# Low-rank attention and a two-layer hard-swish network on one core: transposed scores, sums by a matmul with ones, x kept in SBUF, and the next batch's attention woven between the layers

## The chip, the cores and the metric

One core of one Trainium2 chip runs the whole program. The metric is the device time in microseconds (us), as the median of several runs. A profile of one execution comes with each kernel; its span is some 2 us shorter than the timed run. In the profile PE is the matrix engine, PEld its weight loads, DVE the vector engine, ACT the scalar engine, POOL GpSimd, and L106 is line 106 of that kernel's file. In these kernels PE's products go to tiles in PSUM, the weights and the tiles of k, v, q and x lie in SBUF, and DRAM is the memory that the loads come from.

## The reference, cut to what matters

```python
# attention: batch 8, heads 8, seq 1024, head_dim 64, k_proj 64
k_proj = einsum('ks,bhsd->bhkd', E, k)          # E, F: 64 x 1024
v_proj = einsum('ks,bhsd->bhkd', F, v)
scores = (q @ k_proj^T) / 8;  attn = softmax(scores)      # over 64 columns
x = (attn @ v_proj) transposed to (8192 tokens, 512)
# two layers: 512 -> 2048 -> 512
h = x @ w_in
g = h * clip(h + 3, 0, 6) / 6
out = g @ w_out                                  # 8192 x 512, float32
```

## The kernel before

Attention for all eight batches comes first and writes x to DRAM; then the layers run on blocks of 512 tokens. Inside a batch the probabilities have tokens on partitions, so the row sums are a DVE reduction, and the probabilities have to be divided and then transposed before the product with the values.

```python
kv_pool = tile_pool(name="kv", bufs=1)           # one buffer each for k, q, v
for b in range(B):
    for name, dram in kqv_dram.items():          # rows of 64 floats, 256 bytes
        for so in range(SO):
            load_bf16(t[:, so, :, :], dram[b, :, so])
    ...                                          # projections, q transposes, scores
    nc.scalar.activation(sc_sb[:, h], sc_ps, AF.Exp, scale=scale)
    nc.vector.tensor_reduce(den, sc_sb, axis=AX.X, op=ALU.add)
    nc.vector.reciprocal(den, den)
    nc.vector.tensor_mul(sc_sb, sc_sb, den[:, :, :, None].broadcast_to(...))
    ...                                          # 64 transposes of sc_sb into aT_sb
    nc.tensor.matmul(av_ps, vp_all[:, h, :], aT_sb[...])
    nc.scalar.copy(av_full[:, h, ...], av_ps)
    nc.sync.dma_start(out=xsc_av2[b], in_=av_full)          # x to DRAM
for b in range(B):
    do_moe(b)                                    # reads x from DRAM, and per block:
#   for fo in range(16): 4 matmuls; scalar.copy(h_sb, h_ps);
#       vector.tensor_scalar(t_sb, h_sb, +3, max 0); tensor_scalar(min 6, /6); tensor_mul(g, t_sb, h_sb)
#   for tc_i in range(4): 16 matmuls with g; scalar.copy(o_sb, o_ps); store
```

The softmax here doesn't subtract the row's maximum and nothing guards it: scores larger than these inputs give would overflow.

## Time and profile before

| | before |
|---|---|
| time, median (range) | 749.39 us (748.07 to 750.86) |
| profiled span | 748.0 us |
| attention, until the first layer starts | about 289 us |
| layers, 16 blocks of 28.39 us | about 454 us |
| busy: PE, DVE, ACT, POOL | 80%, 53%, 38%, 24% |
| mean granted clock | 0.906 |

The slices and stretches, which the prediction shows, are read first: they say in which stage an engine is full. Here that is PE, at full clock, in the layers; in attention no engine stays full. Then one reads the chain of waits for the pace of the full stage.

### The profile page before, as it was taken

To read this page: it belongs to the slowest core of one execution; us is meant where nothing else is said; L and a number is where in the kernel's file an instruction comes from. 1 tells how busy PE (TensorE), PEld (TensorE's weight loads), DVE (VectorE), ACT (ScalarE), POOL (GpSimd) and SP (SyncE) were. 2 spreads that over 40 slices of the span, in tenths; PEclk is the share of its full clock that TensorE was granted. 3 is DMA by queue.
4 is the path that set the end of the run, shared out by engine and by line. 5 is a ranking of instruction groups with operands and counts; after the bars stand their busy time and mean duration, and the time that the engine had idled before them with its cause. 6 is when DMAs were issued, how large, how long until landed. Compare 5 with 4: busy or idle time off the path is not lost.

```text
span 748.0 us, 9892 instructions
## 1 busy us (share of the span) xinstructions
PE 597.5 (80%) x3751; PEld 307.4 (41%) x3792; DVE 395.7 (53%) x1040; ACT 283.5 (38%) x513; POOL 180.7 (24%) x220
## 2 busy tenths in 40 slices
PE   0446393663935739999999999999999999999997
PEld 0225263342633524444444444444444444444443
DVE  0146657466584675473473473573563563663652
ACT  0023241632515426354353353353353352452451
POOL 5994676568675600000000000000000000000000
PEclk9986676766867668999999999999999999999999
DMA  9999999999999922211111111111102102101011
GB/s 169 171 155 83 179 145 171 134 132 150 128 154 126 120 57 57 71 42 57 69 44 57 56 57 58 57 43 71 57 32 82 56 29 85 56 30 57 14 43 57
DMA packets 224655, 63.82 MB, mean 85 GB/s; under 512 B 201440, under 2 KB 211680, under 8 KB 224608
## 3 DMA queue, kind: packets, MB, share of 16 engines
q0 software_dynamic: 202720, 29.64, 56.3%
q1 hardware_dynamic: 21888, 33.56, 14.7%
q8 instruction: 29, 0.48, 0.2%
q14 instruction: 18, 0.15, 0.1%
HBM read 67.63 MB, written 25.17 MB: 124 GB/s over the span
## 4 chain that ended last, share of the span: by engine, by line
DVE 31%; PE 27%; issue 4%; ACT 2%; ACTq 0%; DVEq 0%
PE p L119 23%; DVE g_sb L115 14%; DVE t_sb L113 10%; DVE t_sb L111 7%; PE p L106 4%; ACT h_sb L109 1%; ACT av_full L213 1%; ACT sc_sb L189 0%; ACT o_sb L122 0%; ACTq L109 0%; DVEq L115 0%
## 5 line engine op out<-in xcount | busy, mean ns | idle before, releaser
L119 PE MATMUL p<-w_out_sb,g_sb 128*128 128x512 bf16 x1003 | 224.9, 379 | 10.0 <-DVE g_sb L115 8.9
L106 PE MATMUL p<-x_sb,w_in_sb 128*128 128x512 bf16 x1004 | 223.9, 381 | 1.3 <-issue 0.2
L109 ACT CAST h_sb<-p 128x512 bf16<-128x512 f32 x256 | 150.1, 587 | 70.8 <-PE p L106 54.2
L111 DVE TENSOR_SCALAR t_sb<-h_sb 128x512 bf16<-128x512 bf16 x256 | 73.4, 287 | 194.0 <-ACT h_sb L109 193.8
L119 PEld LDWEIGHTS <-g_sb 128*128 128x128 bf16 x1024 | 99.0, 98 | 133.5 <-DVE g_sb L115 18.1
L106 PEld LDWEIGHTS <-w_in_sb 128*128 128x128 bf16 x1024 | 100.5, 98 | 122.5 <-issue 2.8
L201 PE MATMUL p<-ident,sc_sb 128*64 128x128 bf16 x512 | 44.6, 272 | 96.9 <-DVE sc_sb L194 96.9
L115 DVE TENSOR_TENSOR g_sb<-t_sb,h_sb 128x512 bf16<-128x512 bf16 x256 | 108.8, 425 | 9.4
L122 ACT COPY o_sb<-p 128x512 f32<-128x512 f32 x64 | 37.5, 586 | 194.3 <-PE p L119 185.7
L213 ACT CAST av_full<-p 64x512 bf16<-64x512 f32 x128 | 62.6, 616 | 124.6 <-issue 92.6
L201 PEld LDWEIGHTS <-sc_sb 128*64 128x64 bf16 x512 | 43.4, 147 | 97.8 <-DVE sc_sb L194 85.1
L113 DVE TENSOR_SCALAR t_sb<-t_sb 128x512 bf16<-128x512 bf16 x256 | 75.2, 294 | 8.5
L63 POOL DMA_DIRECT2D k<-in_k_dram x64 | 56.3, 934 | 36.8 <-PE p L147 36.7
L63 POOL DMA_DIRECT2D v<-in_v_dram x64 | 56.9, 939 | 27.8 <-DMA k<-in_k_dram 26.8
L189 ACT ACTIVATE sc_sb<-p 128x512 bf16<-128x512 f32 x64 | 32.2, 624 | 71.0 <-PE p L184 49.7
L63 POOL DMA_DIRECT2D q<-in_q_dram x64 | 56.6, 983 | 0.3 <-PE p L201 0.3
L203 DVE COPY aT_sb<-p 64x512 bf16<-64x512 bf16 x128 | 48.4, 412 | 6.5 <-PE p L201 5.9
L192 DVE TENSOR_REDUCE den<-sc_sb 128x64 f32<-128x4096 bf16 x8 | 35.4, 4420 | 24.4 <-ACT sc_sb L189 24.4
L209 PE MATMUL p<-aT_sb,vp_all 64*64 64x512 bf16 x128 | 35.5, 376 | 3.7
L194 DVE TENSOR_TENSOR sc_sb<-sc_sb,den 128x4096 bf16<-128x4096 bf16 x8 | 35.4, 4424 | 0.3
L152 DVE CAST ktp_all<-p 128x64 bf16<-128x64 f32 x32 | 6.9, 224 | 39.7 <-PE p L147 39.7
L155 PE MATMUL p<-v,F_sb 128*64 128x512 bf16 x64 | 24.4, 524 | 2.3 <-DMA v<-in_v_dram 2.3
(28 smaller groups left out, 166.4 us busy)
## 6 DMA issues: line engine op xcount, KB each, us to landing
out_dram<-o_sb SPq DMA_DIRECT2D x64, 256.0 KB, 2.0
k<-in_k_dram POOLq DMA_DIRECT2D x64, 128.0 KB, 9.8
v<-in_v_dram POOLq DMA_DIRECT2D x64, 128.0 KB, 6.3
q<-in_q_dram POOLq DMA_DIRECT2D x64, 128.0 KB, 6.1
x_scratch<-av_full SPq DMA_DIRECT2D x8, 1024.0 KB, 9.2
x_sb<-x_scratch SPq DMA_DIRECT2D x16, 512.0 KB, 3.4
w_in_sb<-in_moe_w_in_dram POOLq DMA_DIRECT2D x4, 512.0 KB, 7.7
w_out_sb<-in_moe_w_out_dram POOLq DMA_DIRECT2D x16, 128.0 KB, 4.9
```

What stands on the lines that cost most here:

```text
L63: nc.gpsimd.dma_start(out=dst, in_=src)
L106: nc.tensor.matmul(h_ps, w_in_sb[:, ko, fo * P:(fo + 1) * P], x_sb[:, ko, :], start=(ko == 0), stop=(ko == KO - 1))
L109: nc.scalar.copy(h_sb, h_ps)
L111: nc.vector.tensor_scalar(t_sb, h_sb, scalar1=3.0, scalar2=0.0, op0=ALU.add, op1=ALU.max)
L113: nc.vector.tensor_scalar(t_sb, t_sb, scalar1=6.0, scalar2=1.0 / 6.0, op0=ALU.min, op1=ALU.mult)
L115: nc.vector.tensor_mul(g_sb[:, fo, :], t_sb, h_sb)
L119: nc.tensor.matmul(o_ps, g_sb[:, fo, tc_i * P:(tc_i + 1) * P], w_out_sb[:, fo, :], start=(fo == 0), stop=(fo == FO - 1))
L122: nc.scalar.copy(o_sb, o_ps)
L201: nc.tensor.transpose(aT_ps[:, ss * P:(ss + 1) * P], sc_sb[:, h, so, :], ident)
L203: nc.vector.tensor_copy(aT_sb[:, h, sg * 4:(sg + 1) * 4, :].rearrange("p a b -> p (a b)"), aT_ps)
L209: nc.tensor.matmul(av_ps, vp_all[:, h, :], aT_sb[:, h, sg * 4:(sg + 1) * 4, :].rearrange("p a b -> p (a b)"), start=True, stop=True)
L213: nc.scalar.copy(av_full[:, h, sg * 512:(sg + 1) * 512], av_ps)
```

## The change

The intent is to take out the serial steps of attention, and to give PE, which is in order and the bound of the layers, an unbroken program in which attention's waits lie behind matmuls of the layers.

```diff
-    "k": k.rearrange("b h (so si) d -> b si so h d", si=P),     # 256-byte rows, 8 transfers, bufs=1
+    "k": k.rearrange("b h (si so) d -> b si h so d", so=SO),    # 2 KB rows, one transfer, bufs=2
...
+  # scores transposed: projected keys on partitions, tokens on the free axis; kb is block-diagonal
+  nc.tensor.matmul(ps, kb[:, 2 * j + a, :], qT[j][:, a, :], start=True, stop=True)
+  nc.scalar.activation(aT[j][:, a, :], ps, AF.Exp, scale=scale)
+  # four 64x64 matmuls on four different quarters of the array
+  for t in range(NB):
+      for a in range(2):
+          r, c = t * KP, a * D
+          nc.tensor.matmul(tiles[t][c:c + D], stationary(r, 2 * j + a), aT[j][r:r + KP, a, :], ...)
+  den = quads(lambda r, h: ones[r:r + KP, :], j);  av = quads(lambda r, h: vp[r:r + KP, h, :], j)
+  # 1/den as exp(-ln(den)) on ACT, one product on DVE, x stays in SBUF
+  nc.scalar.activation(lns[t], den[t], AF.Ln)
+  nc.scalar.activation(rec, ln, AF.Exp, scale=-1.0)
+  nc.vector.tensor_mul(xT[:, j, t, :], av, rec)
...
-  nc.scalar.copy(h_sb, h_ps)                    # then three DVE passes
+  nc.scalar.activation(r, h_ps, AF.Relu, bias=half[:], scale=1.0 / 6.0)
+  nc.vector.scalar_tensor_tensor(g[:, fo, :], r, 1.0, h_ps, op0=ALU.min, op1=ALU.mult)
...
+  for t in range(NB):                           # two blocks per batch
+      for fo in range(FO):
+          first_group(xT, t, g, fo)
+          next(steps, None)                     # one step of the next batch's attention
+          if prev is not None and fo % SB == SB - 1:
+              second_group(*prev, fo // SB)     # a quarter of the block before
+              next(steps, None)
+      prev = (b, t, g)
```

Instructions are issued in the order of the program text; no scheduler moves them. The order of the loads is: k, v, q of batch 0, w_in, w_out, k, v, q of batch 1.

More of the change, by code (lines that the diff above doesn't have):

```diff
@@ L12 @@
 ALU = mybir.AluOpType
-AX = mybir.AxisListType
 @with_exitstack
@@ L38 @@
     FO = d_ff // P
-    x_scratch = nc.dram_tensor("x_scratch", (B, d_model, S), bf16, kind="Internal").ap()
-    k_v = k.rearrange("b h (so si) d -> b h si so d", si=P)
-    v_v = v.rearrange("b h (so si) d -> b h si so d", si=P)
-    q_v = q.rearrange("b h (so si) d -> b so si h d", si=P)
+    TOK = 512
+    NB = S // TOK
+    SB = SO // NB
+    kqv_dram = {
+        "k": k.rearrange("b h (si so) d -> b si h so d", so=SO),
+        "v": v.rearrange("b h (si so) d -> b si h so d", so=SO),
+        "q": q.rearrange("b h (si so) d -> b si h so d", so=SO),
+    }
@@ L45 @@
     w_in_v = moe_w_in.rearrange("(ko ki) n -> ki ko n", ki=P)
-    w_out_v = moe_w_out.rearrange("(ko ki) n -> ki ko n", ki=P)
-    x_scratch_v = x_scratch.rearrange("b (ko ki) t -> b ki ko t", ki=P)
-    xsc_av = x_scratch.rearrange("b (h d) (sc si) -> b d h sc si", d=D, si=P)
+    w_out_v = moe_w_out.rearrange("(fo ki) n -> ki fo n", ki=P)
+    out_v = out.rearrange("(b si so) m -> b si so m", si=P, so=SO)
     consts = ctx.enter_context(tc.tile_pool(name="consts", bufs=1))
-    psum = ctx.enter_context(tc.tile_pool(name="psum", bufs=8, space=bass.MemoryType.PSUM))
@@ L54, in ps @@
-    def ps(pp, ff, dt=f32):
-        t = psum.tile([P, 512], f32, tag="p", name="p")
-        if dt != f32:
-            t = t.bitcast(dt)
-        return t[:pp, :ff]
-    _LETTERS = "abcdefgh"
-    def load_bf16(dst, src, eng=None, pool=None, sz=512):
-        nc.gpsimd.dma_start(out=dst, in_=src)
-    ident = consts.tile([P, P], bf16)
-    make_identity(nc, ident)
-    E_sb = consts.tile([P, SO, KP], bf16)
-    F_sb = consts.tile([P, SO, KP], bf16)
-    w_in_sb = consts.tile([P, KO, d_ff], bf16)
@@ L71 @@
-    w_out_sb = consts.tile([P, FO, d_model], bf16)
-    for ko in range(KO):
-        load_bf16(w_in_sb[:, ko, :], w_in_v[:, ko, :], sz=2048)
-    for fo in range(FO):
-        load_bf16(w_out_sb[:, fo, :], w_out_v[:, fo, :], sz=2048)
-    E_raw = consts.tile([KP, SO, P], bf16)
-    F_raw = consts.tile([KP, SO, P], bf16)
-    load_bf16(E_raw, E.rearrange("kp (so si) -> kp so si", si=P), sz=2048)
-    load_bf16(F_raw, F.rearrange("kp (so si) -> kp so si", si=P), sz=2048)
-    for so in range(SO):
-        tp = ps(P, KP, bf16)
-        nc.tensor.transpose(tp, E_raw[:, so, :], ident[:KP, :KP])
-        nc.vector.tensor_copy(E_sb[:, so, :], tp)
-        tp = ps(P, KP, bf16)
-        nc.tensor.transpose(tp, F_raw[:, so, :], ident[:KP, :KP])
-        nc.vector.tensor_copy(F_sb[:, so, :], tp)
@@ L89 @@
-    kv_pool = ctx.enter_context(tc.tile_pool(name="kv", bufs=1))
-    proj_pool = ctx.enter_context(tc.tile_pool(name="proj", bufs=2))
-    work_pool = ctx.enter_context(tc.tile_pool(name="work", bufs=2))
-    av_pool = ctx.enter_context(tc.tile_pool(name="av", bufs=2))
-    moe_x = ctx.enter_context(tc.tile_pool(name="moe_x", bufs=3))
-    moe_g = ctx.enter_context(tc.tile_pool(name="moe_g", bufs=1))
-    moe_o = ctx.enter_context(tc.tile_pool(name="moe_o", bufs=4))
-    TOK = 512
-    def do_moe(b):
-        for tblk in range(S // TOK):
-            x_sb = moe_x.tile([P, KO, TOK], bf16, tag="x_sb")
-            nc.sync.dma_start(out=x_sb[:], in_=x_scratch_v[b, :, :, tblk * TOK:(tblk + 1) * TOK])
-            g_sb = moe_g.tile([P, FO, TOK], bf16, tag="g_sb")
-            for fo in range(FO):
-                h_ps = ps(P, TOK)
-                for ko in range(KO):
-                    nc.tensor.matmul(h_ps, w_in_sb[:, ko, fo * P:(fo + 1) * P], x_sb[:, ko, :],
-                                     start=(ko == 0), stop=(ko == KO - 1))
-                h_sb = moe_o.tile([P, TOK], bf16, tag="hb")
-                nc.scalar.copy(h_sb, h_ps)
-                t_sb = moe_o.tile([P, TOK], bf16, tag="hs")
-                nc.vector.tensor_scalar(t_sb, h_sb, scalar1=3.0, scalar2=0.0,
-                                        op0=ALU.add, op1=ALU.max)
-                nc.vector.tensor_scalar(t_sb, t_sb, scalar1=6.0, scalar2=1.0 / 6.0,
-                                        op0=ALU.min, op1=ALU.mult)
-                nc.vector.tensor_mul(g_sb[:, fo, :], t_sb, h_sb)
-            for tc_i in range(TOK // P):
-                o_ps = ps(P, d_model)
-                for fo in range(FO):
-                    nc.tensor.matmul(o_ps, g_sb[:, fo, tc_i * P:(tc_i + 1) * P],
-                                     w_out_sb[:, fo, :], start=(fo == 0), stop=(fo == FO - 1))
-                o_sb = moe_o.tile([P, d_model], f32, tag="o_sb")
-                nc.scalar.copy(o_sb, o_ps)
-                tok_lo = b * S + tblk * TOK + tc_i * P
-                nc.sync.dma_start(out=out[tok_lo:tok_lo + P, :], in_=o_sb)
@@ L126 @@
-    NPAIR = H // 2
-    kqv_dram = {
-        'k': k.rearrange("b h (so si) d -> b si so h d", si=P),
-        'v': v.rearrange("b h (so si) d -> b si so h d", si=P),
-        'q': q.rearrange("b h (so si) d -> b si so h d", si=P),
-    }
-    xsc_av2 = x_scratch.rearrange("b (h d) s -> b d h s", d=D)
-    for b in range(B):
-        kqv = {}
-        for name, dram in kqv_dram.items():
-            t = kv_pool.tile([P, SO, H, D], bf16, tag=name, name=name)
-            for so in range(SO):
-                load_bf16(t[:, so, :, :], dram[b, :, so])
-            kqv[name] = t
-        k_sb, v_sb, q_sb = kqv['k'], kqv['v'], kqv['q']
-        ktp_all = proj_pool.tile([P, NPAIR, KP], bf16, tag="ktp")
-        vp_all = proj_pool.tile([KP, H, D], bf16, tag="vp")
-        for j in range(NPAIR):
-            ktp_ps = ps(P, KP)
-            for so in range(SO):
-                nc.tensor.matmul(
-                    ktp_ps,
-                    k_sb[:, so, 2 * j:2 * j + 2, :].rearrange("p h d -> p (h d)"),
-                    E_sb[:, so, :],
-                    start=(so == 0), stop=(so == SO - 1))
-            nc.vector.tensor_copy(ktp_all[:, j, :], ktp_ps)
-        vp_ps = ps(KP, H * D)
-        for so in range(SO):
-            nc.tensor.matmul(
-                vp_ps,
-                F_sb[:, so, :],
-                v_sb[:, so, :, :].rearrange("p h d -> p (h d)"),
-                start=(so == 0), stop=(so == SO - 1))
-        nc.vector.tensor_copy(vp_all.rearrange("k h d -> k (h d)"), vp_ps)
-        av_full = av_pool.tile([D, H, S], bf16, tag="av")
-        qT_sb = work_pool.tile([P, NPAIR, SO, P], bf16, tag="qT")
-        sc_sb = work_pool.tile([P, H, SO, KP], bf16, tag="sc")
-        aT_sb = work_pool.tile([KP, H, SO, P], bf16, tag="aT")
-        den = work_pool.tile([P, H, SO], f32, tag="den")
-        for j in range(NPAIR):
-            for sg in range(2):
-                qT_ps = ps(P, 512, bf16)
-                for ss in range(4):
-                    so = sg * 4 + ss
-                    nc.tensor.transpose(
-                        qT_ps[:, ss * P:(ss + 1) * P],
-                        q_sb[:, so, 2 * j:2 * j + 2, :].rearrange("p h d -> p (h d)"),
-                        ident)
-                nc.vector.tensor_copy(
-                    qT_sb[:, j, sg * 4:(sg + 1) * 4, :].rearrange("p a b -> p (a b)"),
-                    qT_ps)
-        for h in range(H):
-            j, hl = h // 2, h % 2
-            off = hl * D
-            sc_ps = ps(P, SO * KP)
-            for so in range(SO):
-                nc.tensor.matmul(
-                    sc_ps[:, so * KP:(so + 1) * KP],
-                    qT_sb[off:off + D, j, so, :],
-                    ktp_all[off:off + D, j, :],
-                    start=True, stop=True)
-            nc.scalar.activation(
-                sc_sb[:, h], sc_ps.rearrange("p (so k) -> p so k", so=SO),
-                AF.Exp, scale=scale)
-        nc.vector.tensor_reduce(den, sc_sb, axis=AX.X, op=ALU.add)
-        nc.vector.reciprocal(den, den)
-        nc.vector.tensor_mul(sc_sb, sc_sb,
-                             den[:, :, :, None].broadcast_to([P, H, SO, KP]))
-        for h in range(H):
-            for sg in range(2):
-                aT_ps = ps(KP, 512, bf16)
-                for ss in range(4):
-                    so = sg * 4 + ss
-                    nc.tensor.transpose(aT_ps[:, ss * P:(ss + 1) * P],
-                                        sc_sb[:, h, so, :], ident)
-                nc.vector.tensor_copy(
-                    aT_sb[:, h, sg * 4:(sg + 1) * 4, :].rearrange("p a b -> p (a b)"),
-                    aT_ps)
-        for h in range(H):
-            for sg in range(2):
-                av_ps = ps(D, 512)
-                nc.tensor.matmul(
-                    av_ps, vp_all[:, h, :],
-                    aT_sb[:, h, sg * 4:(sg + 1) * 4, :].rearrange("p a b -> p (a b)"),
-                    start=True, stop=True)
-                nc.scalar.copy(av_full[:, h, sg * 512:(sg + 1) * 512], av_ps)
-        nc.sync.dma_start(out=xsc_av2[b], in_=av_full)
@@ L216 @@
-    for b in range(B):
-        do_moe(b)
+    kqv_pool = ctx.enter_context(tc.tile_pool(name="kqv", bufs=2))
+    att = ctx.enter_context(tc.tile_pool(name="att", bufs=2))
+    xpool = ctx.enter_context(tc.tile_pool(name="x", bufs=2))
+    gpool = ctx.enter_context(tc.tile_pool(name="g", bufs=2))
+    rpool = ctx.enter_context(tc.tile_pool(name="r", bufs=4))
+    opool = ctx.enter_context(tc.tile_pool(name="o", bufs=3))
+    ps_mm = ctx.enter_context(tc.tile_pool(name="ps_mm", bufs=4, space=bass.MemoryType.PSUM))
@@ new lines, with pmm, pat @@
+    ps_at = ctx.enter_context(tc.tile_pool(name="ps_at", bufs=4, space=bass.MemoryType.PSUM))
+    ctx.enter_context(tc.manual_schedule())
+    def pmm():
+        return ps_mm.tile([P, TOK], f32, tag="mm", name="mm")
+    def pat():
+        return ps_at.tile([P, TOK], f32, tag="at", name="at")
+    nc.scalar.preload_act_table_set("natural_log_exp_and_others")
+    ef_raw = consts.tile([P, S], bf16, name="ef_raw")
+    nc.gpsimd.dma_start(out=ef_raw[:KP], in_=E)
+    nc.gpsimd.dma_start(out=ef_raw[KP:], in_=F)
@@ new lines, in load, with load_kqv @@
+    def load(b, name):
+        t = kqv_pool.tile([P, H, SO, D], bf16, tag=name, name=name)
+        nc.gpsimd.dma_start(out=t, in_=kqv_dram[name][b])
+        return t
+    def load_kqv(b):
+        return {n: load(b, n) for n in ("k", "v", "q")}
+    ident = consts.tile([P, P], bf16, name="ident")
+    make_identity(nc, ident)
+    ones = consts.tile([P, D], bf16, name="ones")
+    nc.vector.memset(ones, 1.0)
+    half = consts.tile([P, 1], f32, name="half")
+    nc.vector.memset(half, 0.5)
+    kbd = [consts.tile([P, H, P], bf16, name=f"kbd{i}") for i in range(2)]
@@ new lines @@
+    for t in kbd:
+        nc.vector.memset(t, 0.0)
+    kqv = {0: load_kqv(0)}
+    w_in_sb = consts.tile([P, KO, d_ff], bf16, name="w_in_sb")
+    w_out_sb = consts.tile([P, FO, d_model], bf16, name="w_out_sb")
+    NW = 4
+    for i in range(NW):
+        c = slice(i * d_ff // NW, (i + 1) * d_ff // NW)
+        nc.gpsimd.dma_start(out=w_in_sb[:, :, c], in_=w_in_v[:, :, c])
+    for i in range(NW):
+        c = slice(i * FO // NW, (i + 1) * FO // NW)
+        nc.gpsimd.dma_start(out=w_out_sb[:, c, :], in_=w_out_v[:, c, :])
@@ new lines, with attention, project, q_transpose @@
+    kqv[1] = load_kqv(1)
+    ef_t = consts.tile([P, 2, SO, 2, KP], bf16, name="ef_t")
+    ef_si = ef_raw.rearrange("r (si so) -> r so si", so=SO)
+    ef_ps = pat().bitcast(bf16)
+    for so in range(SO):
+        nc.tensor.transpose(ef_ps[:, so * P:(so + 1) * P], ef_si[:, so, :], ident)
+    ef_pv = ef_ps.rearrange("p (so e r) -> p e so r", so=SO, e=2)
+    for e in range(2):
+        for a in range(2):
+            nc.vector.tensor_copy(ef_t[:, e, :, a, :], ef_pv[:, e])
+    def attention(b, xT):
+        kt, vt, qt = kqv[b]["k"], kqv[b]["v"], kqv[b]["q"]
+        kb = kbd[b % 2]
+        def project(e, src):
+            ps = pat()
+            for so in range(SO):
+                nc.tensor.matmul(ps, ef_t[:, e, so].rearrange("p a m -> p (a m)"), src[:, :, so, :],
+                                 start=(so == 0), stop=(so == SO - 1))
+                if so == SO // 2 - 1:
+                    yield
+            res[e] = ps
+        res = {}
+        yield from project(0, kt)
+        kp = att.tile([KP, H, 2, D], bf16, tag="kp", name="kp")
+        k_ps = res[0].rearrange("p (h d) -> p h d", h=H)
+        for a in range(2):
+            nc.vector.tensor_copy(kp[:, :, a, :], k_ps[:KP])
+        yield
+        yield from project(1, vt)
+        vp = att.tile([P, H, D], bf16, tag="vp", name="vp")
+        nc.vector.tensor_copy(vp.rearrange("p h d -> p (h d)"), res[1])
+        yield
+        kt_ps = pat().bitcast(bf16)[:, :H * KP]
+        for h in range(H):
+            nc.tensor.transpose(kt_ps[:, h * KP:(h + 1) * KP], kp[:, h].rearrange("p a d -> p (a d)"),
+                                ident[:KP, :KP])
+        kt_ps = kt_ps.rearrange("p (h m) -> p h m", h=H)
+        nc.vector.tensor_copy(kb[:D, :, :KP], kt_ps[:D])
+        nc.vector.tensor_copy(kb[D:, :, KP:], kt_ps[D:])
+        yield
+        qT, aT = {}, {}
+        def q_transpose(j):
+            ps = pat().bitcast(bf16)
+            for a in range(2):
+                for m in range(SB):
+                    o = (a * SB + m) * P
+                    nc.tensor.transpose(ps[:, o:o + P],
+                                        qt[:, 2 * j + a, 2 * m:2 * m + 2, :].rearrange("p s d -> p (s d)"),
+                                        ident)
+            qT[j] = att.tile([P, 2, TOK], bf16, tag="qT", name="qT")
+            nc.vector.tensor_copy(qT[j].rearrange("p a n -> p (a n)"), ps)
+        def scores(j):
+            aT[j] = att.tile([P, 2, TOK], bf16, tag="aT", name="aT")
+            for a in range(2):
+                ps = pat()
+                nc.tensor.matmul(ps, kb[:, 2 * j + a, :], qT[j][:, a, :], start=True, stop=True)
+                nc.scalar.activation(aT[j][:, a, :], ps, AF.Exp, scale=scale)
+        def quads(stationary, j):
+            tiles = [pat() for t in range(NB)]
+            for t in range(NB):
+                for a in range(2):
+                    r, c = t * KP, a * D
+                    nc.tensor.matmul(tiles[t][c:c + D], stationary(r, 2 * j + a),
+                                     aT[j][r:r + KP, a, :], start=True, stop=True)
+            return tiles
+        def values(j):
+            den = quads(lambda r, h: ones[r:r + KP, :], j)
+            av = quads(lambda r, h: vp[r:r + KP, h, :], j)
+            lns = []
+            for t in range(NB):
+                lns.append(att.tile([P, TOK], f32, tag="ln", name="ln"))
+                nc.scalar.activation(lns[t], den[t], AF.Ln)
+            return av, lns
+        def normalise(j, t, av, ln):
+            rec = att.tile([P, TOK], f32, tag="rec", name="rec")
+            nc.scalar.activation(rec, ln, AF.Exp, scale=-1.0)
+            nc.vector.tensor_mul(xT[:, j, t, :], av, rec)
+        q_transpose(0)
+        yield
+        for j in range(KO):
+            scores(j)
+            yield
+            if j + 1 < KO:
+                q_transpose(j + 1)
+            yield
+            yield
+            av, lns = values(j)
+            yield
+            for t in range(NB):
+                normalise(j, t, av[t], lns[t])
+                yield
@@ new lines, in first_group, with second_group @@
+    def first_group(xT, t, g, fo):
+        h_ps = pmm()
+        for ko in range(KO):
+            nc.tensor.matmul(h_ps, w_in_sb[:, ko, fo * P:(fo + 1) * P], xT[:, ko, t, :],
+                             start=(ko == 0), stop=(ko == KO - 1))
+        r = rpool.tile([P, TOK], f32, tag="r", name="r")
+        nc.scalar.activation(r, h_ps, AF.Relu, bias=half[:], scale=1.0 / 6.0)
+        nc.vector.scalar_tensor_tensor(g[:, fo, :], r, 1.0, h_ps, op0=ALU.min, op1=ALU.mult)
+    def second_group(b, t, g, c):
+        o_ps = pmm()
+        for fo in range(FO):
+            nc.tensor.matmul(o_ps, g[:, fo, c * P:(c + 1) * P], w_out_sb[:, fo, :],
+                             start=(fo == 0), stop=(fo == FO - 1))
+        o_sb = opool.tile([P, d_model], f32, tag="o_sb", name="o_sb")
+        nc.scalar.copy(o_sb, o_ps)
+        nc.sync.dma_start(out=out_v[b, :, NB * c + t, :], in_=o_sb)
@@ new lines, in x_tile @@
+    def x_tile():
+        return xpool.tile([P, KO, NB, TOK], bf16, tag="xT", name="xT")
+    xT = x_tile()
+    for _ in attention(0, xT):
+        pass
+    prev = None
+    for b in range(B):
+        steps = iter(())
+        if b + 1 < B:
+            x_next = x_tile()
+            steps = attention(b + 1, x_next)
+        if b + 2 < B:
+            kqv[b + 2] = load_kqv(b + 2)
+        for t in range(NB):
+            g = gpool.tile([P, FO, TOK], bf16, tag="g", name="g")
+            for fo in range(FO):
+                first_group(xT, t, g, fo)
[4 more added lines that the diff above has]
+            prev = (b, t, g)
+        for _ in steps:
+            pass
+        if b + 1 < B:
+            xT = x_next
@@ L221 @@
+    for c in range(SB):
+        second_group(*prev, c)
 _INS = ['q', 'k', 'v', 'E', 'F', 'moe_w_in', 'moe_w_out']
```

## The prediction

> **What bounds the kernel now.** I read the slices of the page first, then the busy time by stretches, then the chain of waits in order of time, then the groups by form, then the waits. The slices show two stages:
>
> ```profile
> PE   0446393663935739999999999999999999999997
> DVE  0146657466584675473473473573563563663652
> ACT  0023241632515426354353353353353352452451
> POOL 5994676568675600000000000000000000000000
> PEclk9986676766867668999999999999999999999999
> DMA  9999999999999922211111111111102102101011
> ```
>
> Attention for all eight batches comes first, then the two layers. The stretches (PE, weight load, DVE, ACT, POOL, clock, DMA, GB/s):
>
> ```profile
> 20.00:22.00 2.00, 0.00 (x0) 0.00 (x0) 0.00 (x0) 0.00 (x0) 1.64 (x4) 1.00 1.24 202
> 35.00:40.00 5.00, 3.50 (x6) 0.65 (x5) 0.05 (x1) 0.00 (x0) 5.00 (x7) 1.00 2.43 155
> 100.00:150.00 50.00, 30.16 (x365) 20.35 (x363) 28.07 (x48) 23.31 (x48) 32.56 (x38) 0.75 1.74 149
> 400.00:450.00 50.00, 48.55 (x222) 21.84 (x225) 29.71 (x96) 22.29 (x38) 0.00 (x0) 1.00 0.16 53
> ```
>
> Up to about 289 us no engine is full and the granted clock is about 0.75: loads in 256-byte rows, one buffer for k, q and v, and a serial chain inside a batch. After that PE is 97% busy at full clock. The chain gives the pace there:
>
> ```profile
> 375.28 0.88 PE p L106 x4
> 403.67 0.88 PE p L106 x4
> 432.06 0.88 PE p L106 x4
> 534.89 10.53 PE p L119 x48
> ```
>
> One block of 512 tokens takes 403.67 - 375.28 = 28.39 us, and 16 blocks take 454 us. The last row gives the pace of one full matmul, (10.53 - 0.38) / 47 = 0.216 us, where 0.38 is the latency of the last. 128 of them are 27.65, so 0.74 of a block is waiting, mostly for the last g_sb. The durations I use (busy, mean ns):
>
> ```profile
> L109 ACT CAST h_sb<-p 128x512 bf16<-128x512 f32 x256 | 150.1, 587 | 70.8 <-PE p L106 54.2 <-DVE t_sb L113 8.3 <-DVE g_sb L115 4.2
> L189 ACT ACTIVATE sc_sb<-p 128x512 bf16<-128x512 f32 x64 | 32.2, 624 | 71.0 <-PE p L184 49.7 <-issue 21.3
> L160 DVE CAST vp_all<-p 64x512 bf16<-64x512 f32 x8 | 5.5, 683 | 24.2 <-PE p L155 24.2
> L176 DVE COPY qT_sb<-p 128x512 bf16<-128x512 bf16 x64 | 22.2, 408 | 4.8 <-PE p L172 4.7
> ```
>
> And from the timeline, 32 transposes at full clock, (1.96 - 0.23) / 31 = 0.056 us each, and the wait that attention's serial chain puts on PE:
>
> ```profile
> 262.61 1.96 PE L172 MATMUL p<-ident,q 128*128 128x128 bf16 x32
> PE p L201 <- DVE sc_sb L194: 96.9, 8, 12.6
> ```
>
> **What the Trainium skill says.** "TensorE: Matmul & The Clock Gate", Part 1: a clock gate follows recent activity, half rate after an idle window of about 3.4 us and full after a busy one. The trace agrees: 0.75 in attention, 1.00 in the layers. So woven attention should run at full clock. "TensorEngine Tiling (Array Packing)", Tiling Modes and Key Properties: a 64x64 shape is four independent tiles, and a change of mode drains the array. The trace has 64x64 matmuls, but all on one tile, so it shows neither. "DMA: Bandwidth & Descriptors", Specifications: rows under 512 B do not reach line rate. The trace agrees: 155 GB/s written with 256-byte source rows, 202 with the 2 KB rows of w_out. "ScalarE: Activation LUTs", Table sets: one set holds both exp and ln. The built program has one table load; the kernel before uses no ln, so it shows nothing more.
>
> **The change, part by part.**
> Removed: the 96.9 us in which PE waits for the division by row sums, the transposes of the probabilities, the trip of x through DRAM, and DVE's three passes per group (0.29 + 0.29 + 0.42 us) for one that reads PSUM.
>
> Layers: 2048 full matmuls stay. With the second layer one block behind, the 0.74 us per block should vanish: 2048 x 0.216 = 442.4 us.
>
> Attention on PE, per batch: two projections, 16 x 0.216 = 3.46; the key transposes, 8 of 64 columns, about 0.03 each, 0.25; the q transposes, 32 x 0.056 = 1.79; the scores, 8 x 0.216 = 1.73; sums and values, 32 matmuls of 64x64, in groups of four different tiles. One after the other they are 32 x 0.216 = 6.91; perfectly overlapped 1.73. I take pairs, 3.46 (my estimate, as the weight loads of two tiles in the same rows may block each other). Entering and leaving the small mode 8 times costs the latency beyond the pace, 0.38 - 0.216 = 0.16, so 1.3. Sum 12.0 us, on the path for the seven woven batches: 84.0.
>
> Start: batch 0's attention, batch 1's loads. The queue carries in order E and F (0.26 MB written), k, v, q of batch 0 (3.15), both weights (4.19), and k, v, q of batch 1 (3.15), in all 10.75 MB. At 201 GB/s from 2.5 us on (first bytes in the trace), plus 1.1 us to the semaphore (E_raw landed at 25.1 after 4.33 MB), q of batch 1 lands at 53.5 + 2.5 + 1.1 = 57 us. Batch 0's q lands near 23 us; its attention, four head pairs at about 4.7 us (six activations of 0.62 and one round through PE), ends near 44. Then PE's program needs k of batch 1 after the first group of layer one, at about 47, v after the third, q after the sixth. PE runs in program order, so by 57 it has done only 24 matmuls of the layers, the projections and the key transposes of batch 1. From there it should not stop.
>
> Sum: 57 + (2048 - 24) x 0.216 = 437 + (84.0 - 3.7) = 80 + end 4 (the last matmul before started at 744.0 of 748.0) + 3 for a cold clock when PE restarts + 4 for local waits = 585 us.
>
> ACT and DVE lie beside this. ACT: 256 + 8 x 24 activations of 0.62 and 64 copies of 0.59 make 316 us. DVE: 256 passes of 0.69, per batch 8 products of 0.69, three PSUM casts of 0.68, two copies of 0.41 and four of 0.66 (1024 wide) make 265 us. Both are under 60% of the span.
>
> **Rivals.**
> 1. The four tiles run one after another. For it: no overlap is seen before. Against: the skill. It adds 7 x 3.45 = 24, so 609; full overlap takes off 12, so 573.
> 2. The start is longer, because the large kqv loads move at the old 155 GB/s: 10.75 MB take 69 us in place of 53.5, so 600. Against: w_out has the same 2 KB rows and got 202.
> 3. DVE takes the place of PE locally: in the two normalising steps of a head pair it has 2 x 0.69 us against 0.865 of PE, so it falls 1 us behind, 28 times, and PSUM fills: up to +28, so 613. Against: four PSUM buffers are 2.6 us of lead, and every fourth group is followed by 3.5 us of second-layer matmuls without DVE work.
> 4. Attention hides entirely, as if the layers had idle PE time to fill: 57 + 437 + 10 = 504. Against: PE is 97% busy there, so every woven matmul lengthens the path.
>
> **Range and chances.** The large gain is safe: 289 us of attention become about 57 of start and 80 of woven matmuls. Overlap (-12 to +24), DMA rate (up to +15) and local waits (-4 to +15) give the range 565 to 612. They rarely all go one way. Faster by over 2% has 0.98.
>
> **What would show it.** PE busy over 95% and clock 1.00 from about 60 us to the end; PE waiting for k, v, q loads before 60; layer matmuls still 0.216 apart; the group of eight sum and value matmuls taking about 0.9 us (1.7 if serial, 0.45 to 0.6 if overlapped); 64 to 68 us per batch in the steady part and 55 in the last, which has no attention; PE waits for PSUM released by DVE under 10 us. Wrong if PE's longest waits in the steady part are on DVE or ACT, or if the loads of batch 1 land after 65.

## The result

The changed kernel takes 575.71 us (574.86 to 576.98, 4 runs) against 749.39 (748.07 to 750.86, 4 runs). The ratio is 0.7688, with a 95% interval of 0.7668 to 0.7707. Ratios are the mean time of one kernel's fast runs over that of the other's in the same rounds, so not quite the ratio of the medians. Run again later on another occasion it took 576.09 (ratio 0.7693); differences below are against that.

The slices after, in the order of the page:

```profile
PE   2656999999999999999999999999999999999997
DVE  1342764354535454535544454345444544444420
ACT  0261876366644665356743576437653666544431
PEclk9887999999999999999999999999999999999999
DMA  9999992552419150380507333000110000011011
```

A slice is now 14.3 us. Four slices of start are left; after them PE is full and the clock is full. In stretches (PE, PEld, DVE, ACT, POOL, clock, DMA, GB/s) there are the bad piece of the start, one whole batch with attention woven in, and the last batch, which has none:

```profile
40.00:50.00 10.00, 1.79 (x5) 0.69 (x6) 0.69 (x1) 0.59 (x1) 0.00 (x0) 0.50 1.24 207
218.30:284.56 66.26, 65.10 (x346) 29.64 (x352) 31.39 (x49) 37.52 (x66) 2.63 (x3) 1.00 0.41 80
496.45:551.71 55.26, 55.00 (x253) 25.05 (x256) 22.03 (x33) 26.68 (x40) 0.00 (x0) 1.00 0.10 39
```

The difference of the last two rows, 66.26 - 55.26 = 11.0 us, is what attention costs per batch. The 55.26 are 256 matmuls at 0.216. The period is the distance between equal pieces in the chain of waits, here of the second layer:

```profile
218.30 2.75 PE mm L223 x12
284.56 2.75 PE mm L223 x12
350.82 2.75 PE mm L223 x12
417.08 2.75 PE mm L223 x12
```

PE's timeline around the end of batch 0's attention (start, duration, engine, line; the dots stand for rows left out) shows the standstill:

```profile
37.28 0.97 PE L214 MATMUL mm<-xT,w_in_sb 128*128 128x512 bf16 x2 [0.16 <-issue]
39.28 0.58 PE L214 MATMUL mm<-xT,w_in_sb 128*128 128x512 bf16 x1 [1.04 <-DVE xT L193]
48.21 1.89 PE L126 MATMUL at<-k,ef_t 128*128 128x512 bf16 x4 [8.34 <-DMA k<-in_k_dram]
...
53.33 1.04 PE L126 MATMUL at<-v,ef_t 128*128 128x512 bf16 x4
...
58.37 0.62 PE L159 MATMUL at<-ident,q 128*128 128x128 bf16 x8
```

The bracket at the end of the third row tells what came before it: 8.34 us idle until k of batch 1 has landed. Everything earlier is loads and batch 0's attention. The last two rows are the first work on v and q of batch 1. Each starts within 0.1 us of its landing, which the trace puts at 53.29 and 58.32. In the steady part, one visit to the sums and values (the eight small matmuls of a head pair) looks like this:

```profile
207.14 0.41 PE L177 MATMUL at<-aT,ones 64*64 64x512 bf16 x4
207.38 0.39 PE L177 MATMUL at<-aT,vp 64*64 64x512 bf16 x4
207.70 1.90 PE L214 MATMUL mm<-xT,w_in_sb 128*128 128x512 bf16 x7
```

Four matmuls with 512 columns each start and give way to the next four within 0.24 us, where one after another they would need 4 x 0.216 = 0.86. The groups that took the place of the three DVE passes, and the longest PE wait for another engine:

```profile
L218 DVE SCALAR_TENSOR_TENSOR g<-r,mm 128x512 bf16<-128x512 f32 x256 | 175.5, 686 | 227.4 <-ACT r L217 226.8
L217 ACT ACTIVATE r<-mm,half 128x512 f32<-128x512 f32 x256 | 176.8, 691 | 73.6 <-PE mm L214 72.0
PE at L169 <- DVE qT L163: 6.2, 8, 0.8
```

DVE is idle for long stretches in front of its group, waiting for ACT, and ACT in front of its own, waiting for PE, so neither is the bound. The last row says that PE waits for DVE's first copy of q once per batch, 6.2 us in the whole run.

### The profile page after: what moved, and what is told of

It reads as the page before. It is cut to its first block, busy times and chain, and to the rows that moved or that the text cites. A ratio compares the mean times of both kernels' runs of the same rounds, so it can differ in the third digit from the quotient of the medians.

```text
span 573.1 us, 7173 instructions
## 1 busy us (share of the span) xinstructions
PE 532.7 (93%) x2770; PEld 240.3 (42%) x2824; DVE 254.4 (44%) x400; ACT 302.9 (53%) x513; POOL 28.9 (5%) x40
## 4 chain that ended last, share of the span: by engine, by line
PE 86%; DMA 8%; DVE 2%; ACT 1%; issue 1%; POOL 1%; ACTq 0%; POOLq 0%
PE mm L223 38%; PE mm L214 37%; DMA v<-in_v_dram 4%; PE at L126 4%; DMA w_in_sb<-in_moe_w_in_dram 4%; PE at L177 3%; PE at L169 2%; PE at L159 2%; DVE g L218 1%; ACT r L217 1%; DVE qT L163 1%; PE at L145 0%; POOL v L78 0%; POOL q L78 0%; POOL k L78 0%
## 5 line engine op out<-in xcount | busy, mean ns | idle before, releaser
L218 DVE SCALAR_TENSOR_TENSOR g<-r,mm 128x512 bf16<-128x512 f32 x256 | 175.5, 686 | 227.4 <-ACT r L217 226.8
L214 PE MATMUL mm<-xT,w_in_sb 128*128 128x512 bf16 x982 | 241.2, 381 | 3.0 <-DVE xT L193 1.0
L223 PE MATMUL mm<-w_out_sb,g 128*128 128x512 bf16 x1012 | 230.0, 379 | 0.6
L217 ACT ACTIVATE r<-mm,half 128x512 f32<-128x512 f32 x256 | 176.8, 691 | 73.6 <-PE mm L214 72.0
L223 PEld LDWEIGHTS <-g 128*128 128x128 bf16 x1024 | 99.8, 98 | 119.3
L226 ACT COPY o_sb<-mm 128x512 f32<-128x512 f32 x64 | 37.5, 587 | 164.7 <-PE mm L223 161.9
L193 DVE TENSOR_TENSOR xT<-at,rec 128x512 bf16<-128x512 f32 x64 | 43.5, 685 | 22.1 <-ACT rec L192 22.1
L192 ACT ACTIVATE rec<-ln 128x512 f32<-128x512 f32 x64 | 40.6, 641 | 0.0
L126 PE MATMUL at<-k,ef_t 128*128 128x512 bf16 x64 | 18.8, 426 | 14.4 <-DMA k<-in_k_dram 14.4
L78 POOL DMA_DIRECT2D k<-in_k_dram x8 | 7.0, 881 | 140.6 <-PE at L126 137.0
L78 POOL DMA_DIRECT2D q<-in_q_dram x8 | 7.0, 880 | 140.1 <-PE at L159 136.0
```

The lines of the kernel that those rows point to most:

```text
L126: nc.tensor.matmul(ps, ef_t[:, e, so].rearrange("p a m -> p (a m)"), src[:, :, so, :], start=(so == 0), stop=(so == SO - 1))
L192: nc.scalar.activation(rec, ln, AF.Exp, scale=-1.0)
L193: nc.vector.tensor_mul(xT[:, j, t, :], av, rec)
L214: nc.tensor.matmul(h_ps, w_in_sb[:, ko, fo * P:(fo + 1) * P], xT[:, ko, t, :], start=(ko == 0), stop=(ko == KO - 1))
L217: nc.scalar.activation(r, h_ps, AF.Relu, bias=half[:], scale=1.0 / 6.0)
L218: nc.vector.scalar_tensor_tensor(g[:, fo, :], r, 1.0, h_ps, op0=ALU.min, op1=ALU.mult)
```

## The experiments

The theory to be tested: the time is the start, until PE has data for an unbroken program, plus PE's program in order at 0.216 us per full matmul; what the other engines and the DMA do beside it is hidden. Its rivals: the gain is that of the removed work, and the weaving matters little; or another engine is already about to be the bound.

All runs gave the right result. Times are medians of four runs; "more" or "less" is against 576.09. The experiments were run on three occasions, each on another chip, and the kernel before, timed beside them, took 749.71, 748.68 and 747.80 us. So a difference of under 2 us between runs of different occasions says little.

### Weaving undone

```diff
-            steps = attention(b + 1, x_next)
+            for _ in attention(b + 1, x_next):
+                pass
```

> The next batch's attention is issued whole ahead of the batch's layers, not woven in; everything else as in the changed kernel. Theory: the work on PE is the same 11 us per batch, but each batch now shows its chain through ACT and DVE: about 15 us from q transposes to the last product as in batch 0 plus 7 to 9 for projections, so 12 to 14 us more for each of 7 batches, and colder clock: 655 to 675. Rival (the gain came from the removed work, not from the weaving): under 600.

Measured: 647.44 us, ratio 0.8654, so 71 us more; somewhat less than the expected range. One period, with attention alone and then the layers alone:

```profile
192.99:212.95 19.96, 15.28 (x97) 6.46 (x97) 9.35 (x15) 11.73 (x23) 2.62 (x3) 0.78 0.88 139
212.95:268.76 55.81, 55.54 (x250) 25.17 (x255) 23.28 (x34) 27.45 (x42) 0.00 (x0) 0.99 0.16 45
```

Attention by itself takes 20.0 us at a clock of 0.78, woven in it costs 11.0. Per period that is 75.77 - 66.26 = 9.5 us, 67 in seven batches. The expectation had taken 7 to 9 us for the projections and 15 for the chain from the q transposes on. In the trace the first part takes 3.9 us (192.99 to 196.87) and the second 16.1, so the shortfall lies in the projections. Of the 173 us between the two kernels, about 71 come from the weaving, as measured by taking it out of the finished kernel. The other 102 come without it, from the removed work and the other parts together.

### Four small tiles made into full matmuls

Zero-padded weights of 128x128, two matmuls accumulating into each output, so the same count of instructions and the same result. The padding costs three more small DVE copies per batch.

```diff
-  nc.tensor.matmul(tiles[t][c:c + D], stationary(r, 2 * j + a), aT[j][r:r + KP, a, :], start=True, stop=True)
+  nc.tensor.matmul(tiles[t], stationary(t, a), aT[j][:, a, :], start=(a == 0), stop=(a == 1))
```

> The sums and values without small tiles: zero-padded 128x128 weights, the same 32 matmuls per batch, two accumulating into each output, same result. Theory: eight of them take 8 x 0.216 = 1.73 us instead of the 0.56 in the trace, 4 x 7 times on PE's path: +33 us, about 608. Rival (PE has waits in the attention steps that the longer matmuls fill): less than +15.

Measured: 605.74 us, ratio 0.8077, 30 more. The same visit in its trace, and two pieces that give its period:

```profile
219.16 1.03 PE L192 MATMUL at<-aT,ones 128*128 128x512 bf16 x4
220.02 1.03 PE L192 MATMUL at<-aT,vbd 128*128 128x512 bf16 x4
220.88 1.89 PE L229 MATMUL mm<-xT,w_in_sb 128*128 128x512 bf16 x7
...
232.54 2.75 PE mm L238 x12
303.06 2.75 PE mm L238 x12
```

The visit takes 1.72 us in place of 0.56, and the period is 70.52, 4.26 more, 29.8 in seven batches. PE's path explains the whole difference, and the extra DVE copies do not lie on it: PE's waits for qT are 6.9 us, against 6.2. It is a little less than 28 x 1.16 = 32.5, because the small visits also cost some 0.09 us before they begin, which the full ones do not.

### The sums issued twice

```diff
-            for t in range(NB):
+            for t in list(range(NB)) * times:      # times = 2 for the sums
```

> The four small matmuls of the sums are issued twice per head pair, with the same result. Theory (four tiles overlap, 0.24 us per four): 28 x 0.24 = +6.7, about 582.5. Rival (they run one after another, and the trace's spacing is a drawing): 28 x 0.86 = +24, about 600.

Measured: 581.55 us, ratio 0.7779, 5.5 more. Four more small matmuls in each of 28 woven visits cost 0.2 us each time, so the overlap is real and not a drawing of the profile.

### The loads of batch 1 ahead of the second layer's weights

```diff
+    kqv[1] = load_kqv(1)
     for i in range(NW):
         nc.gpsimd.dma_start(out=w_out_sb[:, c, :], in_=w_out_v[:, c, :])
-    kqv[1] = load_kqv(1)
```

> Only change: k, v, q of batch 1 are loaded ahead of w_out instead of behind it. Theory (the time is the start until PE has its data, plus PE's program in order): the three tensors land 10.5 us earlier, PE no longer stands still from 39.9 to 48.2 us and w_out still arrives before its first use at about 63, so 9 to 11 us less than 575.7: about 566. Rival (the start is bound by batch 0's own attention and its activations, the loads lie beside it): at most 3 us less, above 572.

Measured: 567.33 us, ratio 0.7573, 8.8 less, just under the expected 9 to 11. PE waits for k only once, for batch 0's, at the very start (6.9 us; in the changed kernel two waits, 14.4). Batch 1's first projection now starts at 41.70, right behind batch 0's last wait (41.32), so it is batch 0's attention that bounds the start from here.

### The same, and one empty step in each batch

```diff
         q_transpose(0)
         yield
+        yield
         for j in range(KO):
```

> The same reordering, and one empty step more between the first q transposes and the first scores of every batch, so that the DVE copy of qT is done when PE comes to it. Theory: the 0.79 us wait per batch goes away, 7 times, so about 5 us less than the reordering alone: 560. Rival: the wait only moves to a later step or PSUM, no difference to the reordering alone (within 1.5 us).

Measured: 561.24 us, ratio 0.7487, 6 less again. Its only wait for qT is that of batch 0, and its period is 65.40:

```profile
PE at L169 <- DVE qT L163: 0.8, 1, 0.8
...
204.14 2.59 PE mm L215 x12
269.54 2.59 PE mm L215 x12
```

This version beats both kernels: 15 us, 2.7% less than the changed one (0.7487 / 0.7693 = 0.973).

### x through DRAM again

x of each batch is written to DRAM and read back before the layers take it, first for all batches, then for all but batch 0.

```diff
+            nc.sync.dma_start(out=x_scratch[b, t], in_=x[:, :, t, :])
+            nc.sync.dma_start(out=y[:, :, t, :], in_=x_scratch[b, t])
```

> x goes to DRAM and back between attention and the layers, as in the kernel before, all else as changed. Theory: the trip of batch b+1 is begun with some eight steps of batch b to spare, about 15 us or more, and takes 5 to 12 us, so it is hidden except for batch 0, where it adds its latency of about 10 us less what the wait for batch 1's loads at 48 us hides: 0 to +5, so 576 to 581. Rival (the DRAM trip was a cost in itself): +15 or more, with PE waiting for x at every batch.

Measured: 588.31 us, ratio 0.7856, 12 more: a miss. The period stayed at 66.26, but PE stood still in the start:

```profile
PE mm L216 <- DMA x<-x_scratch: 21.4, 2, 20.0
...
40.67 1.29 SPq L237 DMA_DIRECT2D x_scratch<-xT  x2
49.86 4.72 SPq L239 DMA_DIRECT2D x<-x_scratch  x2
```

The second pair of rows is the queue of the transfers: the write of x was issued at 40.67, and the read could only be issued at 49.86, when the write had landed; the data came at 58.8. The DMA was full of batch 1's loads at that time, so each of the two halves of x (512 KB) was slow: the first took 9.2 us to DRAM and 8.9 us back. I had put the whole trip at 10.

> x through DRAM and back for batches 1 to 7, batch 0 direct. In the run with all batches the period stayed at 66.26 us and the start alone lost 20 us in a wait for x behind the bulk loads. Theory: the trip is hidden for the later batches, within 2 us of the changed kernel, 574 to 578. Rival (the trip costs in the steady part too): +10 or more.

Measured: 578.27 us, ratio 0.7729, 2.2 more, just outside what was expected; the period is again 66.26. There is one wait for x of 1.6 us. In the steady part, where no bulk load is under way, the read could be issued 3.4 us after the write (158.21 to 161.59), against 9.2 in the start. So keeping x in SBUF is worth nothing that these runs show in the steady part, once attention is a batch ahead, and some 10 us in the start.

### Short rows in the loads

```diff
-        "k": k.rearrange("b h (si so) d -> b si h so d", so=SO),
+        "k": k.rearrange("b h (so si) d -> b si h so d", so=SO),     # and 8 transfers per tensor
```

> k, q and v loaded in 256-byte rows by 8 transfers each, as in the kernel before, tokens in the old order. Theory: only the start sees it: 6.3 MB at 155 in place of 207 GB/s are 10 us more before v of batch 1 is there, +8 to +12, about 586; GpSimd is busy 7 us per tensor but off the path. Rival (the loads also disturb the steady part through DMA or GpSimd): +25 or more, and a period longer than 66.3 us per batch.

Measured: 588.09 us, ratio 0.7856, 12.0 more, at the upper edge of the range. The period is 66.26 (431.02 to 497.28 in its chain), although GpSimd was busy 176 us in place of 29. So the large loads with long rows are worth something in the start alone.

The run changes two things at once, the rows and the number of transfers, and the trace speaks for the second, against the expectation's "off the path". GpSimd needs 7.05 us to issue the eight transfers of k, and between 60 and 75 us it is busy 14.63 of 15.00 us. At some 0.87 us for 128 KB, issuing alone gives 151 GB/s (my estimate from these figures), and 144 to 146 were moved while GpSimd was full. In the kernel before, the 24 transfers of batch 0 (issued from 21.4 to 41.5 us) each land some 5 us after their issue, the last no later than the first, as if none had to queue. Longer rows in as many transfers were not tried, so this stays open.

### The lag of the second layer, and the three passes

First the lag alone undone: the second layer follows its own block's first.

```diff
-                if prev is not None and fo % SB == SB - 1:
-                    second_group(*prev, fo // SB)
-                    next(steps, None)
+            for c in range(SB):
+                second_group(b, t, g, c)
+                next(steps, None)
```

> The second layer directly behind its own block's first layer, not one block behind; the attention steps are called as often, first 16 and then 4 in a block. Theory: PE stands still once a block until the last g is there (ACT 0.69, DVE 0.69, latency, about 1.3 us; it was 0.6 to 0.74 in the kernel before), 16 times: +12 to +22 us, 588 to 598; DVE falling behind in the now denser first layer can add to that. Rival (attention steps fill that gap): under +5.

Measured: 579.4 us, ratio 0.7744, 3.3 more. The theory's number is a miss, and the rival's is right, though for another reason, which I saw only now. The second layer takes g in order, and its last matmul of the first quarter comes 15 x 0.216 = 3.2 us after its first. The last g needs only some 1.4 us (0.69 on ACT and 0.69 on DVE). There is nothing to wait for, with or without a lag, as long as DVE keeps up, and this run's trace has no wait of PE for g. So I undid the single pass, with and without the lag.

```diff
-        nc.scalar.activation(r, h_ps, AF.Relu, bias=half[:], scale=1.0 / 6.0)
-        nc.vector.scalar_tensor_tensor(g[:, fo, :], r, 1.0, h_ps, op0=ALU.min, op1=ALU.mult)
+        nc.scalar.copy(h_sb, h_ps)
+        nc.vector.tensor_scalar(t_sb, h_sb, scalar1=3.0, scalar2=0.0, op0=ALU.add, op1=ALU.max)
+        nc.vector.tensor_scalar(t_sb, t_sb, scalar1=6.0, scalar2=1.0 / 6.0, op0=ALU.min, op1=ALU.mult)
+        nc.vector.tensor_mul(g[:, fo, :], t_sb, h_sb)
```

> Only the step between the layers undone: ACT copies PSUM to bf16 and DVE makes three passes (0.29, 0.29 and 0.42 us, 1.0 in all against 0.69), second layer still one block behind. Theory (every fourth group is followed by 3.5 us of second-layer matmuls, in which DVE catches up, and PSUM buffers hold the rest): within +3 of the changed kernel, 574 to 579. Rival (DVE, with 1.0 us against PE's 0.865 per group plus attention's share, becomes the bound in the woven steps): +15 or more.

Measured with the lag: 580.76 us, ratio 0.7762, 4.7 more, a little over the expected 3. PE's wait for qT grew from 6.2 to 10.1 us, as DVE's queue is longer where attention's copies stand in it.

> The three passes and the second layer directly behind its own block's first. The run without the lag alone cost only 3 us, because the second layer uses g in order and needs the last of it only 3.5 us later. Theory: the wait for g in the kernel before came from DVE being slower than PE over 16 groups in a row; with three passes and attention's DVE work in the same 16 groups it comes back: 16 x 1.0 + 6 or so of attention against 16 x 0.865 + 10 of PE in a block with attention, and as before (0.74) in one without: +8 to +25, 584 to 600. Rival (the lag never mattered): under +5, below 581.

Measured without the lag: 605.13 us, ratio 0.809, 29 more, above the expected range. The old wait is back, 16 times, and attention's copies now hold PE up as well:

```profile
PE at L169 <- DVE qT L163: 13.7, 8, 2.0
PE mm L226 <- DVE g L221: 9.5, 16, 0.6
PE at L177 <- DVE qT L163: 6.1, 7, 1.0
```

These sum to 29.3 us, against 6.2 in the changed kernel, which is most of the difference. The period is 70.35 (366.89 to 437.24), 4.09 more, 28.6 in seven batches. So the lag is worth 3.3 us beside a single DVE pass and 605.13 - 580.76 = 24 beside three; the single pass is worth 4.7 us with the lag and 26 without it. Each does nearly the whole of the work of the other.

### The changed kernel again

> The changed kernel once more, beside its variants on the same chip: 574 to 577 us.

Measured: 576.09 us, ratio 0.7693.

## Why the prediction was right

It said 585 us, with 565 to 612; 575.7 came out. By its steps:

**The layers at 0.216 us, without the 0.74 per block.** Right as a number: 55.26 us per batch without attention, which is 256 x 0.216. The cause it named was only half right. It put the vanished wait down to the lag. The runs show that either the lag or the single DVE pass is enough to remove most of it, and that it returns in full only where both are undone.

**The start.** Right, mechanism and size. It had the loads of k, v and q in turn set the pace, with q at 57 and 24 matmuls of the layers done by then. In the trace k landed at 48.2, v at 53.3 and q at 58.3, and PE had done just those 24 when it began on q at 58.4. The rate was 207 GB/s in the piece shown, where 201 was assumed. Moving the loads gained nearly the 9 us that this reading gives. Batch 0's attention was mis-sized: its last product was done at 39.8, not 44 (the prediction's own figures add to 42), because a head pair took 3.55 us (products at 27.87 and 31.43) and not 4.7. That this did not show is luck: the loads came later still.

**Attention's cost on PE.** The mis-sized term, worked out as 12.0 us per batch and measured as 11.0. Sums and values were put at 3.46 for tiles overlapping in pairs plus 1.3 for entering and leaving, 4.76 in all. They take 4 x 0.65 = 2.6, counting the 0.09 before each visit, because all four overlap and the switching costs about 0.2 per visit. Against that, some 0.8 us of wait for qT per batch lie within the measured 11.0; the prediction had kept 4 us for all local waits apart from its 12.0. With both put in, its sum is 10.6; the last 0.4 is not accounted for.

**The sum.** In the prediction's own terms: 58.3 of start, 2024 x 0.216 = 437.2, 7 x 11.0 less the 3.7 already done = 73.3, and 4 of end make 572.8; the profiled span is 573.1. Against the 585, the attention term with its waits is 84 + 4 - 77 = 11 less, the start 1.3 more, and the 3 for a cold clock fall away: from 51.31 us on four matmuls took 0.86 us again, while PE was still to be held by v and q. The range's lower end, 565, is below what its parts allow (585 - 12 - 4 = 569).

**The signs.** From the restart on they came as written: PE busy 65.10 of 66.26 us at clock 1.00, and periods of 66.26 and 55.26 where 64 to 68 and 55 were named. A visit took 0.56 us, which it had listed as the overlapped case. One sign of being wrong came true by its letter: after 80 us every wait of PE that the trace lists is on DVE, for qT. They are 0.8 us each, 1.2% of a period, so they do not make DVE the bound; the sign should have named a size.

**What it took from the skill.** The woven attention ran at clock 1.00, the four tiles overlapped, and one table load of 1.28 us served both Exp and Ln. The 155 GB/s that it set beside the rule on short rows does not show that rule: GpSimd was busy issuing for all 5.00 us of that stretch.

**Rivals.** The serial tiles fall with the trace and the two runs on them. The slow loads fall: 12 us come back only with the short rows in eight transfers each. DVE as a local bound holds in small: 0.8 us per batch, removed by one empty step, and 29 us where DVE is given its old work and the lag is gone. That attention would be free falls: each batch pays 11.0 us.

Not settled: how the 102 us that come without weaving divide among the transposed scores, the sums by matmul and the second set of buffers. They lean on each other's layouts, and no run undid one of them alone. Nor was it tested how much of the 289 us the loads alone would have held: the DMA row stays at 9 through most of them.

## What to carry to other kernels

Where an in-order engine is the bound of one stage and idles in another, weave the two: the cost of the second falls to its own instructions on that engine (here 20 us to 11), and what remains is to count those instructions and to shorten them. After that, look at what the engine waits for first: loads in the order of first use gave some 9 us, one empty step before a dependent one gave 6. When two parts of a change remove the same wait, undoing either alone shows little, so undo both before calling it worthless.

## What the Trainium skill lacked or had wrong

- "TensorE: Matmul & The Clock Gate", Part 2 (Back-to-back issue gap), gives about 131 ns per matmul as the sustained rate at 512 columns in streams of weight load and matmul. Here such streams go at 216 ns, 256 of them in 55.26 us; the figure of about 216 that it gives for an isolated gap, and in its description of the phases for back-to-back matmuls too, is the one that fits.
- "TensorEngine Tiling (Array Packing)", Key Properties, says that a change of mode drains the array, without a cost. Here eight 64x64 matmuls with 512 columns, entered from and left to full matmuls, took 0.65 us, where two rounds of four overlapped ones would need 0.43 at 0.216 a round, so about 0.2 us per visit. Four tiles at once, two of them in the same rows, overlapped fully (0.24 us).
- In no page that I read: what a transfer needs when issued while bulk loads fill the DMA. Here 512 KB to DRAM took 9.2 us and 512 KB back 8.9, where the same write took 3.4 us without bulk loads.
